# A planned attention-and-MLP kernel: an earlier copy of S, recalibrated load times, key products on two engines, and a new order

## The chip, the cores and the metric

The kernel runs on one core of a Trainium2 chip. A core has a matrix engine (TensorE, PE in the profile; its weight loads are PEld), a vector engine (VectorE, DVE), an activation engine (ScalarE, ACT), GpSimd (POOL) and SyncE (SP), which here only issues transfers. Each engine works through its own queue in order; the engines wait for each other by semaphores. SBUF is the working memory of 128 partitions, PSUM the eight banks that TensorE writes to. The metric is the device time of one execution in microseconds (us).

## What is computed

For each of 4 batches and 4 heads (1088 tokens, head size 32), `phi` turns a query or key into 64 products of two 8-wide projections, and attention is linear in them; a two-matrix MLP with a leaky relu follows.

```python
a = einsum('rd,bhsd->bhsr', S1, x);  b = einsum('rd,bhsd->bhsr', S2, x)      # r = 8
phi(x) = (a_i * b_j), 64 values per token
kv = phi(k)^T v;  z = sum over s of phi(k)
attn = phi(q) kv / (phi(q) z + 1e-6)
x = attn as 4352 tokens by 128
h = x @ w_in;  g = max(h, 0) + alpha * min(h, 0);  out = g @ w_out      # w_in 128x2048
```

## The kernel before

The kernel rewrites the MLP: the leaky relu is `alpha*h` plus `(1 - alpha)*relu(h)`. So `out = x @ W + relu(x @ w_in) @ w_out_bf`, with `W = (w_in * alpha) @ w_out` and `w_out_bf = (1 - alpha) * w_out`. Both are made in the opening: four blocks of w_in are transposed on TensorE (L403), multiplied with alpha on VectorE (L411) or ScalarE (L414) into `winT`, and 16 float32 matmuls (L421) add up W; `w_out_bf` is made in four blocks on GpSimd (L393) or ScalarE (L396), and `w_in_bf` in four casts on ScalarE (L385).

*Keys, per batch* (`keys`, L427): VectorE transposes k in two halves (`kT`, L434), TensorE multiplies with `Sk` (L442), VectorE transposes the result back (`ab`, L449). Then four products `phi` (L457; on VectorE for batch 0, on GpSimd for the others), a Gram block on TensorE (L471), from it `exs` (L478, L479), a small matmul with `G` (L481) and the copy of z into `Wq` (L483). `phi` and v give `kv` (L491), which is copied (`kvs`, L495), transposed (L502) and copied again (`kvw`, L504).

*Queries, in five units* (`queries`, L511; units 0 and 1 are batch 0): transposes of q (`qT`, L518), products with `Wq` (L527), four transposes (`qa`, L533), then the chain `ac` (L548), a sum (L550), plus epsilon (L553), reciprocal (L554), `an` (L555, qa times rd), two products `qf` (L562, called `p_` in the code), two transposes `qp` (L566), and the numerator on TensorE (L579). Unit 0 does this chain on VectorE, the others do the products on GpSimd. The numerator's four blocks are copied to `xT` (L588).

*MLP, in nine groups of 512 tokens* (`mlp`, L594; the last has 256): 16 matmuls with `w_in_bf` (L602), a relu each on ScalarE (L609) or VectorE (L611), 16 matmuls with `w_out_bf` (L615), one with W (L622), a transpose out of PSUM (L627) and four stores. A group needs the units that cover its tokens.

*Order.* Nothing loops at run time. Every piece of work is an `Op` with an engine (or several to choose from, with an estimated length each), a priority, what it depends on and which buffers it takes. `schedule` (L65) picks, again and again, the operation that can start first by its own estimates; among those within 60 ns the one of lowest priority number, from `PRIO` (L28). Loads are planned on one imaginary queue `DQ` with the lengths given to `load` (L316). `SLACK` is added to waits between engines, `STICK` favours staying with one shape on TensorE. The resulting list only sets the order in each engine's queue; at run time an instruction starts when its data and buffer are there and its engine is free. Before TensorE has useful work it multiplies zeros (`zeros`, L352): 16 matmuls first, then fillers that the planner puts into gaps. Loads of later batches stand behind one-element memsets on VectorE (`gate`, L331), so that they start when a given piece of the earlier batch is done.

Of the kernel before, what the change touches and what calls it, by code (L numbers as in the profile page):

```python
# [25 lines left out]

SLACK = {"ACT": 0, "PE": 120, "DVE": 80}
PRIO = {"W": -25831, "wm": -16185, "win": 2590, "wo": -34520, "k": [-30754, -2740, -58459, -37449], "v": [-24647, -6543, 39476, 61086], "q": [-69891, -35754, -36540, -9190, 57445], "d": [-53704, -20334, -22485, -17259, 4159]}  # L28

# [19 lines left out]
class Op:  # L49
    def __init__(self, eng, fn, prio, deps=(), takes=(), frees=(), lat=190, ni=2, cfg="full", glue=None):  # L50
# [3 lines left out]
        self.takes, self.lat, self.ni, self.cfg, self.glue = list(takes), lat, ni, cfg, glue  # L54
# [6 lines left out]
SWITCH, COLD, FILL = 95, 6600, 14000  # L61
STICK = {"PE": 22100}


def schedule(ops, slots, filler=None):  # L65
# [4 lines left out]

    free_at = {"DVE": 900, "PE": 1000, "POOL": 700, "ACT": 700}
    cfg, glued = "full", None
# [19 lines left out]
    while ready:  # L92
        best = None
        known = {}
        for o in ready:
# [43 lines left out]
        if e == "PE" and filler and 4000 < free_at.get(e, 0) < FILL:  # L139
# [4 lines left out]
            if n > 0 and idle:  # L144
# [30 lines left out]
def kernel(  # L175
# [52 lines left out]
    Wq = [sb(f"Wq{b}", [128, 32]) for b in range(B)]  # L228
    oma = sb("oma", [128, NC])
    warm = sb("warm", [128, 256], BF16)  # L230
    kvw = [sb(f"kvw{b}", [128, 2, 128]) for b in range(B)]
# [40 lines left out]
    def dve(n):  # L272
        return (62 + n) / 0.96
# [64 lines left out]


    c_ident = op(("POOL", 700), lambda: make_identity(nc, ident), -900)  # L340

# [18 lines left out]
    c_warm0 = op(("DVE", 300), lambda: nc.vector.memset(warm, 0.0), -950)  # L360
    c_warm = op(("PE", 8 * 427 + 80), lambda: zeros(8, "O"), -900, deps=[c_warm0], ni=32)
    h_rows = Hold(HBANKS)
    c_rt = op(("PE", 300), lambda: nc.tensor.transpose(
        bank[h_rows.got[0]][:, :2 * r], rows, ident[:2 * r, :2 * r]),
# [23 lines left out]
    for i in range(4):  # L388
        s = slice(4 * i, 4 * i + 4)

        def f_wo(e, s=s):
            if e == "POOL":
                nc.gpsimd.tensor_mul(w_out_bf[:, s], w_out_f[:, s], view(oma[:, s], [[1, 4], [0, 128]]))  # L393
# [3 lines left out]
        c_wo.append(op({"POOL": 1050, "ACT": 1180}, f_wo, PRIO["wo"] + i, deps=[L[f"wo{i // 2}"], c_om]))  # L397
    for i in range(4):
# [18 lines left out]
    wm = []  # L417
    for i in range(4):
        def f_wm(i=i):
            for c in range(4 * i, 4 * i + 4):  # L420
                nc.tensor.matmul(bank[hW.got[0]][:, :DM], winT[:, c], w_out_f[:, c], start=(c == 0), stop=(c == NC - 1))  # L421
        wm = [op(("PE", 1000), f_wm, PRIO["wm"] + i, deps=[c_wT[i], L[f"wo{i // 2}"]] + wm, takes=[hW] if i == 0 else [],
                 lat=250, ni=16)]
    c_W = op(("ACT", 250), lambda: nc.scalar.copy(W_bf, bank[hW.got[0]][:, :DM]), PRIO["wm"] + 10, deps=wm, frees=[hW])


    def keys(b, prio, late):  # L427
# [25 lines left out]
        for rr_, h2 in ((0, 0), (0, 1), (1, 0), (1, 1)):  # L453
            def f_ph(e, rr_=rr_, h2=h2):
# [4 lines left out]
                               view(src, [[64, KW], [0, r], [1, r]], 32 * rr_ + 16 * h2 + r))  # L459
            e = {"DVE": dve(KW * R)} if PHI_DVE[b] else {"POOL": 50 + KW * R * 2}  # L460
            ph.append(op(e, f_ph, prio + 3, deps=[t2[rr_]] + ph[:1], takes=[hph] if not ph else [], frees=[hab]))

        hz, hE, hC = Hold(banks), Hold(P_ex), Hold(banks)

        def f_gram():

            for w in (0, 5, 1, 6, 2, 7, 3, 8, 4):
# [4 lines left out]
                                 stop=w in (4, 8), skip_group_check=True)  # L472
        zb = op(("PE", 620), f_gram, prio + 3, deps=t2, takes=[hz], frees=[hab], lat=250, ni=36, cfg="128x64")

# [36 lines left out]
    def queries(u, b, starts, nb, end, prio, late, z_op, kv_op):  # L511
# [34 lines left out]
        def rd():  # L546
            return bufs[hrd.got[0]][:, :H * nb]
        ac = op(("POOL", 170 + 2 * n) if slow else ("DVE", dve(n) + 130), lambda e: side(e).tensor_mul(part(2), part(2), part(0)),  # L548
                prio + 3, deps=ta)
        sm = op(("DVE", dve(n) + (30 if slow else 120)), lambda: nc.vector.reduce_sum(rd(), part(2), axis=mybir.AxisListType.X), prio + 3,  # L550
# [4 lines left out]
        an = op(("POOL", 150 + 1.8 * n) if slow else ("DVE", dve(n) + 130), lambda e: side(e).tensor_mul(  # L555
            part(0), part(0), view(bufs[hrd.got[0]], [[1, H * nb], [0, r]])), prio + 3, deps=[rc], frees=[hrd])
        hqf, hqp = [Hold(P_qf) for _ in range(2)], [Hold(P_qp) for _ in range(2)]
        mu = []
        for rr_ in range(2):
            def f_p(e, rr_=rr_):  # L560
# [3 lines left out]
                                   view(src, [[32, 2 * nb], [0, r], [1, r]], 2 * n * rr_ + r))  # L564
            p_ = op(("POOL", 60 + 1.9 * 4 * n) if slow else ("DVE", dve(4 * n)), f_p, prio + 4, deps=[an], takes=[hqf[rr_]], frees=[hqa])
            mu.append(op(("DVE", dve(4 * n) + 40), lambda rr_=rr_: nc.vector.transpose(  # L566
                bufs[hqp[rr_].got[0]][:, :4 * n], bufs[hqf[rr_].got[0]][:, :4 * n]),
                prio + 5, deps=[p_], takes=[hqp[rr_]], frees=[hqf[rr_]]))
# [122 lines left out]
```

## Time and profile before

| | |
|---|---|
| median of 3 runs | 111.69 us (110.04 to 111.81) |
| the profiled execution | 109.54 us, of which the span from first to last instruction is 107.5 us |
| granted TensorE clock | 1.00 |
| relus on ScalarE / VectorE | 107 / 37 |
| phi of batch 0 on VectorE / GpSimd | 4 / 0 |
| w_out_bf blocks on GpSimd / ScalarE | 2 / 2 |

The page has one line for each engine (busy time, share of the span, instructions), a view of the span in 40 slices, the transfers, the chain of waits that ended last, and the costliest groups of instructions. A group's row gives line, engine, operation, what is written from what (buffer numbers left out), count, then busy time and mean ns of one, then the engine's idle time just before, with what ended it. A row of the timeline gives start, length, engine, line, operation, count, and in brackets the idle time before it and what released it. An instruction's recorded length includes its run-out, so that one may start while the one before it is still shown.

### The profile page before, as it was taken

To read this page: it belongs to the slowest core of one execution; us is meant where nothing else is said; L and a number is where in the kernel's file an instruction comes from. 1 tells how busy PE (TensorE), PEld (TensorE's weight loads), DVE (VectorE), ACT (ScalarE), POOL (GpSimd) and SP (SyncE) were. 2 spreads that over 40 slices of the span, in tenths; PEclk is the share of its full clock that TensorE was granted. 3 is DMA by queue.
4 is the path that set the end of the run, shared out by engine and by line. 5 is a ranking of instruction groups with operands and counts; after the bars stand their busy time and mean duration, and the time that the engine had idled before them with its cause. 6 is when DMAs were issued, how large, how long until landed. Compare 5 with 4: busy or idle time off the path is not lost.

```text
span 107.5 us, 3253 instructions
## 1 busy us (share of the span) xinstructions
PE 101.0 (94%) x1309; PEld 53.9 (50%) x1309; DVE 75.1 (70%) x160; ACT 70.7 (66%) x158; POOL 37.6 (35%) x41
## 2 busy tenths in 40 slices
PE   6969999999999999999999999999999899999960
PEld 4638889444546334456443444644454344444740
DVE  2559999897898879699568965885753444564740
ACT  0046889669760499336985974796769599496730
POOL 4000330089879996019993024930000000000000
PEclk9999999999999999999999999999999999999999
DMA  2999870796600288803550320420041060023143
GB/s 62 340 252 402 297 269 6 224 201 206 207 9 0 60 186 155 326 6 51 107 154 3 56 45 0 64 34 6 12 67 18 0 97 7 0 46 61 26 71 49
DMA packets 22863, 11.24 MB, mean 105 GB/s; under 512 B 19008, under 2 KB 21056, under 8 KB 22848
## 3 DMA queue, kind: packets, MB, share of 16 engines
q1 hardware_dynamic: 21952, 10.95, 39.5%
q8 instruction: 10, 0.16, 0.7%
q10 hardware_dynamic: 896, 0.08, 0.6%
q14 instruction: 5, 0.04, 0.2%
HBM read 8.80 MB, written 2.23 MB: 103 GB/s over the span
## 4 chain that ended last, share of the span: by engine, by line
PE 88%; DMA 4%; ACT 2%; DVE 1%; SPq 1%; issue 1%; ACTq 0%
PE O L615 27%; PE H L602 26%; PE A L579 6%; DMA q_sb<-in_q_dram 4%; PE H L421 4%; PE A L602 3%; PE A L527 3%; PE A L471 2%; PE A L491 2%; PE H L491 2%; PE O L355 2%; PE H L442 2%; PE O L622 2%; PE H L403 1%; PE A L442 1%; ACT rh L609 1%
## 5 line engine op out<-in xcount | busy, mean ns | idle before, releaser
L609 ACT ACTIVATE rh<-H 128x512 bf16<-128x512 f32 (+1 forms) x91 | 48.2, 593 | 10.5 <-PE H L602 10.2
L615 PE MATMUL O<-rh,w_out_bf 128*128 128x512 bf16 (+1 forms) x144 | 40.4, 367 | 0.0
L602 PE MATMUL H<-xT,w_in_bf 128*128 128x512 bf16 (+1 forms) x124 | 38.7, 374 | 0.6 <-ACT rh L609 0.6
L611 DVE TENSOR_SCALAR rh<-H 128x512 bf16<-128x512 f32 (+1 forms) x33 | 21.3, 652 | 9.7 <-PE H L602 8.1
L615 PEld LDWEIGHTS <-w_out_bf 128*128 128x128 bf16 x144 | 13.9, 97 | 17.6 <-issue 5.7
L602 PEld LDWEIGHTS <-w_in_bf 128*128 128x128 bf16 x144 | 13.3, 98 | 15.9 <-issue 3.3
L457 POOL TENSOR_TENSOR phi<-ab 128x576 f32<-128x576 f32 x12 | 13.8, 1177 | 13.1 <-DVE ab L449 13.1
L562 POOL TENSOR_TENSOR qf<-qa 128x1152 f32<-128x1152 f32 (+1 forms) x8 | 15.5, 1952 | 0.2
L627 DVE STREAM_TRANSPOSE oT<-O 128x512 f32<-128x512 f32 (+1 forms) x9 | 6.1, 680 | 9.3 <-PE O L622 9.2
L566 DVE STREAM_TRANSPOSE qp<-qf 128x1152 f32<-128x1152 f32 (+2 forms) x10 | 11.2, 1124 | 0.7 <-POOL qf L562 0.7
L609 ACT ACTIVATE rh<-A 128x512 bf16<-128x512 f32 (+1 forms) x16 | 7.1, 505 | 3.2 <-PE A L602 2.9
L355 PE MATMUL O<-warm 128*128 128x256 bf16 x42 | 7.5, 342 | 1.1 <-DVE warm L360 1.1
L434 DVE STREAM_TRANSPOSE kT<-k_sb 128x544 f32<-128x544 f32 x8 | 5.5, 716 | 2.7 <-DMA k_sb<-in_k_dram 2.7
L533 DVE STREAM_TRANSPOSE qa<-A 128x288 f32<-128x288 f32 (+2 forms) x20 | 6.7, 386 | 0.7 <-PE A L527 0.7
L579 PE MATMUL A<-qp,kvw 32*32 32x288 f32 (+2 forms) x320 | 7.0, 364 | 0.0
L588 ACT CAST xT<-A 128x256 bf16<-128x256 f32 (+3 forms) x12 | 3.4, 345 | 5.3 <-PE A L579 5.3
L518 DVE STREAM_TRANSPOSE qT<-q_sb 128x544 f32<-128x544 f32 (+2 forms) x10 | 5.9, 608 | 0.5 <-DMA q_sb<-in_q_dram 0.5
L355 PEld LDWEIGHTS <-warm 128*128 128x128 bf16 x42 | 4.9, 122 | 2.5 <-DVE warm L360 1.1
L393 POOL TENSOR_TENSOR w_out_bf<-w_out_f,oma 128x512 bf16<-128x512 f32 x2 | 2.1, 1042 | 10.8 <-DMA w_out_f<-in_moe_w_out_dram 10.7
L371 ACT ACT_TABLE_LOAD x1 | 1.3, 1283 | 6.7 <-DVE ST L366 6.7
L385 ACT CAST w_in_bf<-w_in_f 128x512 bf16<-128x512 f32 x4 | 4.6, 1157 | 1.0 <-DMA w_in_f<-in_moe_w_in_dram 1.0
L579 PEld LDWEIGHTS A<-qp,kvw 32*32 32x32 f32 x320 | 3.9, 103 | 2.5 <-issue 1.3
(86 smaller groups left out, 92.8 us busy)
## 6 DMA issues: line engine op xcount, KB each, us to landing
k_sb<-in_k_dram SPq DMA_DIRECT2D x3, 544.0 KB, 4.1
q_sb<-in_q_dram SPq DMA_DIRECT2D x3, 544.0 KB, 3.2
out_dram<-oT SPq DMA_DIRECT2D x20, 64.0 KB, 2.0
v_sb<-in_v_dram SPq DMA_DIRECT2D x8, 144.0 KB, 4.2
v_sb<-in_v_dram SPq DMA_DIRECT2D x8, 128.0 KB, 4.6
w_in_f<-in_moe_w_in_dram SPq DMA_DIRECT2D x2, 512.0 KB, 6.1
w_out_f<-in_moe_w_out_dram SPq DMA_DIRECT2D x2, 512.0 KB, 5.8
k_sb<-in_k_dram SPq DMA_DIRECT2D x2, 272.0 KB, 3.1
```

Of the source, the lines that this page charges most:

```text
L355: nc.tensor.matmul(bank[name][:, :256], warm[:, :128], warm[:, :256], start=True, stop=True)
L457: eng.tensor_mul(bufs[hph.got[0]][:, rr_, :, h2].rearrange("p w (i j) -> p w i j", i=r), view(src, [[64, KW], [1, r], [0, r]], 32 * rr_ + ...
L518: tq.append(op(("DVE", dve(32 * (x1 - x0))), lambda x0=x0, x1=x1: nc.vector.transpose(bufs[hqT.got[0]][:, 32 * (x0 - j0):32 * (x1 - j0)], ...
L533: ta.append(op(("DVE", dve(n)), lambda h=h: nc.vector.transpose(bufs[hqa.got[0]][:, h * n:(h + 1) * n], bank[hA[h].got[0]][:, :n]), prio + ...
L562: side(e).tensor_mul(bufs[hqf[rr_].got[0]][:, :4 * n].rearrange("p (m i j) -> p m i j", i=r, j=r), view(src, [[32, 2 * nb], [1, r], [0, r] ...
L566: mu.append(op(("DVE", dve(4 * n) + 40), lambda rr_=rr_: nc.vector.transpose(bufs[hqp[rr_].got[0]][:, :4 * n], bufs[hqf[rr_].got[0]][:, :4 ...
L579: nc.tensor.matmul(bank[hX[c].got[0]][32 * h:32 * (h + 1), :n], kvw[b][32 * c:32 * (c + 1), i, 32 * h:32 * (h + 1)], view(bufs[hqp[h // 2] ...
L602: hm = op(("PE", n / 2.4 + 3), lambda c=c, hh=hh: nc.tensor.matmul(bank[hh.got[0]][:, :n], w_in_bf[:, c * 128:(c + 1) * 128], xT[:, col0:c ...
L609: nc.scalar.activation(bufs[hr.got[0]][:, :n], bank[hh.got[0]][:, :n], ACTF.Relu)
L611: nc.vector.tensor_scalar_max(bufs[hr.got[0]][:, :n], bank[hh.got[0]][:, :n], 0.0)
L615: nc.tensor.matmul(bank["O"][:, :n], w_out_bf[:, c], bufs[hr.got[0]][:, :n], start=state["n"] == 0, stop=state["n"] == last)
L627: ev = op(("DVE", dve(n)), lambda: nc.vector.transpose(bufs[ho.got[0]][:, :nb].rearrange("p a b -> p (a b)"), bank["O"][:, :n]), prio - 5, ...
```

## The change

It makes these edits at once. The planner gets a new rule: operations marked `port` on VectorE and GpSimd are never planned at the same time as each other. The marks are on `w_out_bf`, `phi`, `ac`, `an` and `p_`. For batch 0 `phi` may be planned on either engine, and for unit 0 `p_` too. The memset of `warm` is planned first, and ScalarE copies 8 columns of it to a new tile `tab`, which nothing reads: its activation table is loaded there. W's 16 matmuls become eight operations of two (they were four of four). Planned lengths change for several loads (w_in's first from 2900 to 1500 ns), the Gram block, `phi` and the transpose of S; so do `SLACK`, `STICK`, the times at which engines are taken to begin, and all of `PRIO`. The list of dependencies of `w_out_bf` on unit 0's last `p_` (a rule for the planner only) goes.

```diff
-SLACK = {"ACT": 0, "PE": 120, "DVE": 80}
-PRIO = {"W": -25831, "wm": -16185, "win": 2590, "wo": -34520, "k": [...], ...}
+SLACK = {"ACT": 80, "PE": 60, "DVE": 30}
+PRIO = {"W": -2429, "wm": -2407, "win": -2437, "wo": -610, "k": [...], ...}
...
-STICK = {"PE": 22100}
+STICK = {"PE": 1000}
...
-    free_at = {"DVE": 900, "PE": 1000, "POOL": 700, "ACT": 700}
+    free_at = {"DVE": 830, "PE": 900, "POOL": 700, "ACT": 700}
...
+                if o.port and e in ("DVE", "POOL"):
+                    t = max(t, free_at.get("PORT", 0))
...
+        if o.port and e in ("DVE", "POOL"):
+            free_at["PORT"] = end
...
-    load("k0a", 1600, lambda: l_k(0, 0, 17))
+    load("k0a", 1750, lambda: l_k(0, 0, 17))
...
-    load("v0", 2200, lambda: l_v(0))
-    load("wi0", 2900, lambda: l_win(0))
-    load("wi1", 1400, lambda: l_win(1))
-    load("wo0", 1400, lambda: l_wout(0))
-    load("wo1", 1400, lambda: l_wout(1))
+    load("v0", 2500, lambda: l_v(0))
+    load("wi0", 1500, lambda: l_win(0))
+    load("wi1", 1300, lambda: l_win(1))
+    load("wo0", 1350, lambda: l_wout(0))
+    load("wo1", 1350, lambda: l_wout(1))
...
+    c_warm0 = op(("DVE", 60), lambda: nc.vector.memset(warm, 0.0), -950)
+    c_tab = op(("ACT", 1300), lambda: nc.scalar.copy(tab, warm[:, :8]), -940, deps=[c_warm0])
...
-    for i in range(4):
+    for i in range(8):
         def f_wm(i=i):
-            for c in range(4 * i, 4 * i + 4):
+            for c in range(2 * i, 2 * i + 2):
                 nc.tensor.matmul(bank[hW.got[0]][:, :DM], winT[:, c], w_out_f[:, c], start=(c == 0), stop=(c == NC - 1))
...
-            e = {"DVE": dve(KW * R)} if PHI_DVE[b] else {"POOL": 50 + KW * R * 2}
-            ph.append(op(e, f_ph, prio + 3, deps=[t2[rr_]] + ph[:1], takes=[hph] if not ph else [], frees=[hab]))
+            e = {"DVE": dve(KW * R), "POOL": 1200} if PHI_DVE[b] else {"POOL": 1200}
+            ph.append(op(e, f_ph, prio + 3, deps=[t2[rr_]] + ph[:1], takes=[hph] if not ph else [], frees=[hab], port=True))
...
-            p_ = op(("POOL", 60 + 1.9 * 4 * n) if slow else ("DVE", dve(4 * n)), f_p, prio + 4, deps=[an], takes=[hqf[rr_]], frees=[hqa])
+            p_ = op(("POOL", 60 + 1.9 * 4 * n) if slow else {"POOL": 60 + 1.9 * 4 * n, "DVE": dve(4 * n)}, f_p, prio + 4, deps=[an],
+                    takes=[hqf[rr_]], frees=[hqa], port=True)
...
-        if not slow:
-
-            for x in c_wo:
-                x.deps.append(p_)
```

What the planner makes of it, by the instructions in each engine's queue. In the opening VectorE now copies `ST`, `Sk` and `Y` directly after the two halves of `kT` and ahead of the transposes of q; it does one `phi` of batch 0 (behind `exs`) and GpSimd three; it copies `kvs` between the reciprocal and `an`. GpSimd's three `phi` are followed by three blocks of `w_out_bf`; ScalarE does one, behind its four casts of w_in, two blocks of `winT` and `kvw`. TensorE runs 4 fillers (not 6) ahead of the first key products, 6 and 6 (not 10 and 8) around the Gram block, and puts 12 of W's matmuls before unit 0's numerator and 4 behind it. Then come unit 1's query products and the first MLP matmul, and behind it batch 1's key products, which stood before both. Further on, unit 1's numerator follows all of group 0 and is followed by batch 2's key products and batch 1's `kv`; unit 2's numerator stands inside group 1 instead of behind it. ScalarE has 97 relus and VectorE 47.

More of the change, by code (lines that the diff above doesn't have):

```diff
@@ L49, with __init__ @@
 class Op:
-    def __init__(self, eng, fn, prio, deps=(), takes=(), frees=(), lat=190, ni=2, cfg="full", glue=None):
+    def __init__(self, eng, fn, prio, deps=(), takes=(), frees=(), lat=190, ni=2, cfg="full", glue=None, port=False):
         self.eng = eng if isinstance(eng, dict) else dict([eng])
@@ L53, in __init__ @@
         self.deps = [d for d in deps if d is not None]
-        self.takes, self.lat, self.ni, self.cfg, self.glue = list(takes), lat, ni, cfg, glue
+        self.takes, self.lat, self.ni, self.cfg, self.glue, self.port = list(takes), lat, ni, cfg, glue, port
         for h in frees:
@@ L229 @@
     oma = sb("oma", [128, NC])
+    tab = sb("tab", [128, 8])
     warm = sb("warm", [128, 256], BF16)
@@ L359, in filler @@
         return Op(("PE", each * n), lambda: zeros(n, name), 0, takes=[h], frees=[h], ni=4 * n)
-    c_warm0 = op(("DVE", 300), lambda: nc.vector.memset(warm, 0.0), -950)
     c_warm = op(("PE", 8 * 427 + 80), lambda: zeros(8, "O"), -900, deps=[c_warm0], ni=32)
     h_rows = Hold(HBANKS)
-    c_rt = op(("PE", 300), lambda: nc.tensor.transpose(
+    c_rt = op(("PE", 100), lambda: nc.tensor.transpose(
         bank[h_rows.got[0]][:, :2 * r], rows, ident[:2 * r, :2 * r]),
@@ L396, in f_wo @@
                     nc.scalar.mul(w_out_bf[:, c], w_out_f[:, c], oma[:, c:c + 1])
-        c_wo.append(op({"POOL": 1050, "ACT": 1180}, f_wo, PRIO["wo"] + i, deps=[L[f"wo{i // 2}"], c_om]))
+        c_wo.append(op({"POOL": 1050, "ACT": 1180}, f_wo, PRIO["wo"] + i, deps=[L[f"wo{i // 2}"], c_om], port=True))
     for i in range(4):
@@ L417 @@
     wm = []
-    for i in range(4):
+    for i in range(8):
         def f_wm(i=i):
-            for c in range(4 * i, 4 * i + 4):
+            for c in range(2 * i, 2 * i + 2):
                 nc.tensor.matmul(bank[hW.got[0]][:, :DM], winT[:, c], w_out_f[:, c], start=(c == 0), stop=(c == NC - 1))
-        wm = [op(("PE", 1000), f_wm, PRIO["wm"] + i, deps=[c_wT[i], L[f"wo{i // 2}"]] + wm, takes=[hW] if i == 0 else [],
-                 lat=250, ni=16)]
+        wm = [op(("PE", 480), f_wm, PRIO["wm"] + i, deps=[c_wT[i // 2], L[f"wo{i // 4}"]] + wm, takes=[hW] if i == 0 else [],
+                 lat=250, ni=8)]
     c_W = op(("ACT", 250), lambda: nc.scalar.copy(W_bf, bank[hW.got[0]][:, :DM]), PRIO["wm"] + 10, deps=wm, frees=[hW])
@@ L472, in f_gram @@
                                  stop=w in (4, 8), skip_group_check=True)
-        zb = op(("PE", 620), f_gram, prio + 3, deps=t2, takes=[hz], frees=[hab], lat=250, ni=36, cfg="128x64")
+        zb = op(("PE", 730), f_gram, prio + 3, deps=t2, takes=[hz], frees=[hab], lat=250, ni=36, cfg="128x64")
         def f_ex():
@@ L555, in queries @@
         an = op(("POOL", 150 + 1.8 * n) if slow else ("DVE", dve(n) + 130), lambda e: side(e).tensor_mul(
-            part(0), part(0), view(bufs[hrd.got[0]], [[1, H * nb], [0, r]])), prio + 3, deps=[rc], frees=[hrd])
+            part(0), part(0), view(bufs[hrd.got[0]], [[1, H * nb], [0, r]])), prio + 3, deps=[rc], frees=[hrd], port=True)
         hqf, hqp = [Hold(P_qf) for _ in range(2)], [Hold(P_qp) for _ in range(2)]
```

4 lines of the change are left out of this document (2 added, 2 removed).

## The prediction

> **What bounds the kernel now.** I read the page first, then the chain of waits, then the timeline of each engine through the opening.
>
> ```profile
> PE 101.0 (94%) x1309; PEld 53.9 (50%) x1309; DVE 75.1 (70%) x160; ACT 70.7 (66%) x158; POOL 37.6 (35%) x41
> ...
> PE 88%; DMA 4%; ACT 2%; DVE 1%; SPq 1%; issue 1%; ACTq 0%
> ```
>
> TensorE is busy all the time and is 88% of the chain, so time can be won in two ways only: useful matmuls begin sooner, or the stream of them has fewer pauses. 94% hides two different things, since part of TensorE's opening is filler on zeros. The opening on VectorE (start, length, instruction):
>
> ```profile
> 5.83 0.77 DVE L518 STREAM_TRANSPOSE qT<-q_sb 128x256 f32<-128x256 f32 x2 [0.51 <-DMA q_sb<-in_q_dram]
> 6.52 0.14 DVE L366 COPY ST<-H 128x16 f32<-128x16 f32 x1
> ...
> 7.70 0.48 DVE L449 STREAM_TRANSPOSE ab<-A 128x288 f32<-128x288 f32 x1 [0.68 <-PE A L442]
> ...
> 8.54 1.38 DVE L457 TENSOR_TENSOR phi<-ab 128x576 f32<-128x576 f32 x2
> 9.93 0.19 DVE L478 TENSOR_TENSOR exs<-A,pick 128x32 f32<-128x32 f32 x1
> ...
> 11.99 1.36 DVE L411 TENSOR_TENSOR winT<-H,al 128x512 f32<-128x512 f32 x2 [0.21 <-PE H L403]
> 13.26 0.90 DVE L533 STREAM_TRANSPOSE qa<-A 128x128 f32<-128x128 f32 x4
> 14.19 0.57 DVE L548 TENSOR_TENSOR qa<-qa 128x128 f32<-128x128 f32 x1
> ...
> 15.61 0.29 DVE L555 TENSOR_TENSOR qa<-qa,rd 128x128 f32<-128x128 f32 x1
> 15.94 1.29 DVE L562 TENSOR_TENSOR qf<-qa 128x512 f32<-128x512 f32 x2
> 17.16 1.29 DVE L566 STREAM_TRANSPOSE qp<-qf 128x512 f32<-128x512 f32 x2
> ```
>
> and on TensorE (filler L355, key products L442, W L421, numerator of unit 0 L579, query products L527, the first three MLP matmuls L602):
>
> ```profile
> 4.80 1.22 PE L355 MATMUL O<-warm 128*128 128x256 bf16 x6
> 6.94 0.72 PE L442 MATMUL A<-kT,Sk 64*32 64x288 f32 x16 [0.92 <-DVE Sk L368]
> ...
> 16.10 2.84 PE L421 MATMUL H<-w_out_f,winT 128*128 128x128 f32 x24
> 18.88 1.07 PE L579 MATMUL A<-qp,kvw 32*32 32x128 f32 x64
> 19.94 1.34 PE L442 MATMUL H<-kT,Sk 64*32 64x288 f32 x16
> 21.21 0.62 PE L527 MATMUL A<-qT,Wq 32*32 32x160 f32 x32
> 21.77 0.89 PE L602 MATMUL H<-xT,w_in_bf 128*128 128x512 bf16 x3
> ...
> 44.39 1.60 PE L579 MATMUL A<-qp,kvw 32*32 32x288 f32 x64
> ```
>
> VectorE hardly rests from 5.83 to unit 0's numerator at 18.88; that chain is the limit of the opening, and MLP work starts at 21.77. After it, the chain of waits gives the price of each TensorE block (start, share of the chain, what):
>
> ```profile
> 30.41 0.22 PE A L502 x2
> ...
> 31.06 0.65 PE A L442 x16
> ...
> 33.32 0.87 PE H L471 x18
> 34.19 1.13 PE A L579 x58
> 35.46 0.50 ACT xT L588 x2
> ...
> 37.13 0.61 ACT rh L609
> ...
> 47.16 1.28 PE H L491 x72
> ...
> 57.74 0.70 PE A L527 x32
> ...
> 96.41 3.24 PE O L615 x15
> ```
>
> An MLP matmul costs 3.24/15 = 0.216 us. From 21.77 to 44.39, 22.6 us, stand 65 of them (14.0), two Gram blocks (1.74), L491 1.28, two L527 (1.4), L442 0.65, L579 1.13, L502 0.22 and some 0.3 for L481: 20.7. So about 1.9 us of this stretch are pauses. The two ACT rows show 1.1 of them: between unit 1's numerator and group 1, TensorE waits for the copies of xT and then for the first relu. The other 0.8 are small waits for relus. The same count from 44.39 to the end gives about 3 us in pauses, none long.
>
> **The change part by part.** *S ahead of q.* S, its masked copy and Y leave the place behind two q transposes that wait for q's landing at 5.83, and follow the k transposes: 6.52 becomes about 5.25, and the first key products 6.94 becomes 5.67. TensorE then runs four fillers of the six (4.80 + 4 x 0.20 = 5.6), so it is free. The q transposes keep their landing. What is late next is w_in:
>
> ```profile
> 6.74 1.28 ACT L371 ACT_TABLE_LOAD   x1 [6.74 <-DVE ST L366]
> ...
> 9.71 1.14 ACT L385 CAST w_in_bf<-w_in_f 128x512 bf16<-128x512 f32 x1 [0.99 <-DMA w_in_f<-in_moe_w_in_dram]
> ```
>
> Its transposes cannot start before 9.71, and VectorE's winT products follow them, so of 1.27 us this part alone delivers none beyond that point. *Early table load* (the copy to tab): ACT waited 0.99 us for w_in anyway; worth 0, and 1.28 if that wait were gone.
>
> *Key products on two engines.* Three of four phi leave VectorE (3 x 0.69 = 2.07 us) and go to GpSimd:
>
> ```profile
> L457 POOL TENSOR_TENSOR phi<-ab 128x576 f32<-128x576 f32 x12 | 13.8, 1177 | 13.1 <-DVE ab L449 13.1
> ...
> L393 POOL TENSOR_TENSOR w_out_bf<-w_out_f,oma 128x512 bf16<-128x512 f32 x2 | 2.1, 1042 | 10.8 <-DMA w_out_f<-in_moe_w_out_dram 10.7
> ```
> ```profile
> 12.41 2.20 POOL L393 TENSOR_TENSOR w_out_bf<-w_out_f,oma 128x512 bf16<-128x512 f32 x2 [10.71 <-DMA w_out_f<-in_moe_w_out_dram]
> ```
>
> The first ab transpose moves from 7.70 to 6.55, behind the q transposes; the phi run from 7.0 to 7.0 + 3 x 1.18 = 10.5. L491, which needs them, stands behind three w_in transposes, the first of them at 9.71 or later, so they are hidden. But the two engines disturb each other. L548 and L555 have the same shape; L555 took 0.29, L548 0.57, and L548 ended at 14.76, just after GpSimd's second w_out product (12.41 + 2.20 = 14.61). I read this as VectorE standing still until GpSimd is through. The one phi left on VectorE stands behind the exs pair: second ab transpose done at 7.45, Gram block 0.9 and hand-over, exs and its sum 0.4, so 8.85. It starts at 9.35 or 10.5 (after GpSimd's second or third), the z copy of 0.15 follows at 10.05 to 11.2, the winT pair (not before 10.4, behind the first w_in transposes) takes 13.26 - 11.99 = 1.27, the qa transposes 0.93: L548 is due at 12.6 to 13.55, against 14.19.
>
> *w_out.* GpSimd now takes three of the four products, not two, and they start when w_out lands, at 12.41, in whatever place the planner put them: nothing else holds them back. Two took 2.20, 0.12 of it between them; three take 3.36. L548 and L555 both fall into that stretch. If VectorE gets its turn between two products: L548 ends at 13.75, the next two w_out products run to 15.95. From L548's end to L555 is 15.61 - 14.76 = 0.85 us, plus the copy of kvs, which moves from ScalarE to this place:
>
> ```profile
> L504 DVE COPY kvw<-A 128x256 f32<-128x256 f32 x2 | 0.8, 412 | 0.0
> ```
>
> 0.41: L555 asks at 15.0 and waits to 15.95, so the moved copy is hidden in that wait (and costs 0.41 without it). Then 0.33 + 1.22 + 1.23 as in the rows brings the numerator to 18.85, against 18.88. The bounds are 17.1, with no standing still (12.6 + 0.27 + 0.85 + 0.41 + 2.78, and a little for the start), and 20.0, where VectorE gets the turn only after all three. I take 18.85: it is nearest to the L548 row. [...] Who comes next when both queue, the trace doesn't show.
>
> *W two at a time.* Still 16 matmuls; four of them now stand behind the numerator: 4 x 2.84/12 = 0.95 that the early ones saved where TensorE waits anyway. So: numerator 18.85 + 1.06, W 0.95, L527 0.56: first MLP matmul at 21.4. Batch 1's key products, before it so far (19.94, stretched from 0.65 to 1.34 by a wait for the k transposes), come right after it: 21.4 + 0.65 = 22.05 against 21.77. **The opening loses 0.3.** ScalarE, with four w_in casts first, then two winT blocks, a copy and one w_out block, ends at 9.71 + 7 x 1.14 + 0.4 = 18.1 if none is longer than the cast shown, before xT is due at 19.9: 0. The table of p_'s engines keeps both on VectorE: 0.
>
> *New order.* Behind unit 1's numerator now stand L442 and L491 of the next batches, 0.65 + 1.28 = 1.93 us, ahead of group 1's first two matmuls, and the Gram block behind those. ScalarE's four xT copies (0.50 for two in the row) end inside, so the 1.1 us of waits go; next to be late is VectorE's Gram operand (below). I keep the 0.8 of small waits: **gain 1.1**, bounds 0 and 1.9. *Relus:* by the instruction order ScalarE has 97 instead of 107, VectorE 47 instead of 37. Of the late 3 us I give this 0.5, **bounds -0.7** (the longer VectorE relu delays its transposes) **and 1.2**.
>
> Sum: -0.3 + 1.1 + 0.5 = 1.3 us off 107.5 of span and off the profiled execution's 109.54: 108.2. That execution is the lowest of the four shown; the median of runs is 111.69, the mean of all four 110.8.
>
> **The rivals.** *No standing still* (L548 was long for another reason): numerator 17.1, 1.75 earlier, total 3.05. For it: only one instruction shows the disturbance. Against: it ends with GpSimd to within 0.15 us.
> *GpSimd keeps the turn* while its queue is full: numerator 20.0, total gain 0.15. For it: no row shows VectorE getting in between two queued GpSimd instructions. Against: two w_out leave 0.12 us between them.
> *VectorE becomes the bound*, and the kernel gets slower. Place: from unit 0's last qp transpose (18.73) to batch 2's ab transposes, which the Gram block behind group 1's first two matmuls needs.
>
> ```profile
> 19.00:36.00 17.00, 16.88 (x374) 8.52 (x372) 15.06 (x43) 10.47 (x27) 13.01 (x14) 1.00 0.48 135
> ```
>
> (Busy times of PE, PEld, DVE, ACT, POOL.) VectorE was at 15.06 of 17. The 38 instructions that the changed order puts there come, at the spacing of the same ones in this stretch, to 15.1 us, with 0.55 of waits for L527 to 34.35. TensorE arrives at 21.4 + 33 x 0.216 + 0.65 + 0.87 + 0.15 + 0.70 + 0.3 of small waits = 31.2, then 1.13 + 1.93 + 0.43 = 34.7. Some 0.3 us are spare. If each of the 38 costs 0.07 more, 2.7 in all, TensorE loses 2.4 and the kernel is slower by 1.1. It decides from 0.3 + 1.3 = 1.6 us of lateness on.
>
> **How the numbers follow.** Chances: the sum 0.52, no standing still 0.20, GpSimd keeps the turn 0.14, VectorE bound 0.09, anything else 0.05. From the mean of four, 110.8 - 1.3 = 109.5, which is the forecast; from the median it would be 110.4, from the profiled one 108.2. Range: low 110.8 - 3.05 - 0.5 = 107.2; high 110.8 + 1.1 = 111.9. The sum's own range (opening as taken, bounds of the other terms) is 108.1 to 111.0. 2%, about what a measurement of this kernel can tell, is 2.2 us, or 109.46 against the median. The sum lies at that edge, because the median was the high end of the four: I give it 0.38 of being beyond, no standing still 0.95, the turn kept 0.10: 0.20 + 0.19 + 0.01 = 0.40 faster. Slower by over 2%: half of VectorE bound and some of the rest, 0.06. Within: 0.54.
>
> **What would show it.** The first key products at 5.7 and GpSimd's phi from 7.0 show the first step. The qa,rd product ending just after a w_out product shows the standing still; a numerator at 17 refutes it, at 20 the turn was kept. TensorE without a pause of over 0.3 us behind unit 1's numerator shows the new order's gain; a wait of the Gram block for ab there shows the VectorE rival. I am wrong if the opening ends far from 21.4, or if pauses after 44 change by over 1 us.

## The result, and the profile after

| | kernel before | changed kernel |
|---|---|---|
| median of 20 runs each | 111.12 us (109.44 to 113.42) | 108.82 us (108.2 to 110.76) |
| the profiled execution | 109.54 us, span 107.5 | 109.73 us, span 107.7 |

The ratio is 0.9871, 95% interval [0.9831, 0.9911]: faster, by less than 2%, some 1.4 us. The medians stand further apart (108.82 / 111.12 = 0.979, 2.3 us), because the ratio leaves out the long executions, and the kernel before has more of them: of 47 that ran beside the experiments, 17 had a mean granted TensorE clock under 0.99 and a median of 111.73 us, the other 30 a median of 109.96; of the changed kernel's 20 none was under 0.993.

The two profiled executions mislead as a pair, for they took equally long. The one before would be the second lowest of that kernel's 20 runs, the one after is the fifth highest of its own. So the profile after answers how each step went, not by how much the kernel gained. Its page (busy time of each engine; then the engines' shares of the chain of waits):

```profile
PE 99.5 (92%) x1289; PEld 53.2 (49%) x1299; DVE 80.2 (74%) x166; ACT 66.9 (62%) x146; POOL 42.5 (40%) x45
...
PE 67%; DMA 16%; DVE 10%; ACT 1%; issue 1%; SPq 1%; ACTq 1%; DVEq 0%
```

TensorE's share of the chain went from 88% to 67%, in favour of transfers and VectorE. The pieces of the chain (start, length, what) say which:

```profile
4.21 6.35 DMA w_in_f<-in_moe_w_in_dram
10.60 0.73 PE H L410 x4
11.35 1.29 DVE winT L418 x2
...
16.53 1.29 DVE qf L569 x2
17.83 1.21 DVE qp L574 x2
19.09 5.74 DMA q_sb<-in_q_dram
24.86 1.37 DVE qT L525 x2
```

Up to unit 0's numerator the chain is w_in's landing and then VectorE; after it, the landing of batch 1's queries, a transfer issued at 19.09. The opening on VectorE (line numbers are those of the changed kernel: `ac` L555, +eps L560, `an` L562):

```profile
5.09 0.14 DVE L373 COPY ST<-H 128x16 f32<-128x16 f32 x1
...
6.70 0.77 DVE L525 STREAM_TRANSPOSE qT<-q_sb 128x256 f32<-128x256 f32 x2 [1.12 <-DMA q_sb<-in_q_dram]
...
8.13 1.01 DVE L386 TENSOR_SCALAR oma<-al 128x16 f32<-128x16 f32 x1
...
9.60 1.26 DVE L464 TENSOR_TENSOR phi<-ab 128x576 f32<-128x576 f32 x1
...
13.49 0.96 DVE L555 TENSOR_TENSOR qa<-qa 128x128 f32<-128x128 f32 x1
...
14.81 0.57 DVE L560 TENSOR_SCALAR rd<-rd 128x16 f32<-128x16 f32 x1
...
15.86 0.63 DVE L562 TENSOR_TENSOR qa<-qa,rd 128x128 f32<-128x128 f32 x1
```

and GpSimd, then TensorE:

```profile
7.92 3.97 POOL L464 TENSOR_TENSOR phi<-ab 128x576 f32<-128x576 f32 x3 [6.23 <-DVE ab L456]
13.27 3.08 POOL L400 TENSOR_TENSOR w_out_bf<-w_out_f,oma 128x512 bf16<-128x512 f32 x3 [1.37 <-DVE qa L540]
```
```profile
5.76 1.11 PE L449 MATMUL A<-kT,Sk 64*32 64x288 f32 x16
...
18.59 1.43 PE L583 MATMUL A<-qp,kvw 32*32 32x128 f32 x64 [0.37 <-DVE qp L574]
19.96 1.16 PE L428 MATMUL H<-w_out_f,winT 128*128 128x128 f32 x8
21.05 0.55 PE L534 MATMUL A<-qT,Wq 32*32 32x160 f32 x32
21.85 0.72 PE L449 MATMUL H<-kT,Sk 64*32 64x288 f32 x16 [0.25 <-issue]
22.61 0.38 PE L606 MATMUL H<-xT,w_in_bf 128*128 128x512 bf16 x1
...
32.51 1.18 PE L583 MATMUL A<-qp,kvw 32*32 32x160 f32 x64
33.61 0.72 PE L449 MATMUL H<-kT,Sk 64*32 64x288 f32 x16
34.12 1.32 PE L498 MATMUL H<-phi,v_sb 64*32 64x64 f32 x72
35.38 0.60 PE L606 MATMUL H<-xT,w_in_bf 128*128 128x512 bf16 x2
...
42.94 1.60 PE L583 MATMUL A<-qp,kvw 32*32 32x288 f32 x64
```
```profile
21.96 0.60 ACT L613 ACTIVATE rh<-H 128x512 bf16<-128x512 f32 x1 [0.54 <-PE A L534]
```

The row at 22.61 is not the first MLP matmul. In the changed order that one stands ahead of batch 1's key products, and its record is missing: the profile has 144 weight loads at L606 but 142 matmuls, the first load is at 21.53, and the relu at 21.96 already reads a result. So the first MLP matmul ran at about 21.63, in the 0.25 us that the row at 21.85 shows as "issue", and 22.61 is the second.

Three things are to be seen. First, q landed at 6.70, not 5.83, and w_in at 10.58, not 9.71 (4.21 + 6.35 by the chain gives 10.56); the change leaves the order of these loads as it was. Second, three VectorE instructions beside GpSimd's products are long: `oma` 1.01 (0.13 in the profile before), `ac` 0.96 and +eps 0.57, against 0.29 and 0.17 for the same shapes alone in the profile before. Third, behind unit 1's numerator TensorE runs on.

### The profile page after: what moved, and what is told of

It reads as the page before. It is cut to its first block, busy times and chain, and to the rows that moved or that the text cites. A ratio compares the mean times of both kernels' runs of the same rounds, so it can differ in the third digit from the quotient of the medians.

```text
span 107.7 us, 3221 instructions
## 1 busy us (share of the span) xinstructions
PE 99.5 (92%) x1289; PEld 53.2 (49%) x1299; DVE 80.2 (74%) x166; ACT 66.9 (62%) x146; POOL 42.5 (40%) x45
## 4 chain that ended last, share of the span: by engine, by line
PE 67%; DMA 16%; DVE 10%; ACT 1%; issue 1%; SPq 1%; ACTq 1%; DVEq 0%
PE O L619 25%; PE H L606 23%; DMA w_in_f<-in_moe_w_in_dram 6%; DMA q_sb<-in_q_dram 5%; PE A L583 5%; DMA rows<-in_S_dram 3%; PE A L606 2%; PE H L498 2%; PE A L534 2%; DMA out_dram<-oT 2%; PE A L478 2%; PE O L626 1%; DVE qT L525 1%; DVE qf L569 1%; PE H L449 1%; DVE winT L418 1%
## 5 line engine op out<-in xcount | busy, mean ns | idle before, releaser
L613 ACT ACTIVATE rh<-H 128x512 bf16<-128x512 f32 (+1 forms) x82 | 44.8, 593 | 14.2 <-PE H L606 12.8
L606 PE MATMUL H<-xT,w_in_bf 128*128 128x512 bf16 (+1 forms) x122 | 37.0, 374 | 0.6 <-ACT rh L613 0.3
L619 PE MATMUL O<-rh,w_out_bf 128*128 128x512 bf16 (+1 forms) x136 | 36.9, 366 | 0.4
L615 DVE TENSOR_SCALAR rh<-H 128x512 bf16<-128x512 f32 (+1 forms) x42 | 27.3, 661 | 5.5 <-PE H L606 4.3
L606 PEld LDWEIGHTS <-w_in_bf 128*128 128x128 bf16 x144 | 13.4, 98 | 17.0 <-issue 4.7
L464 POOL TENSOR_TENSOR phi<-ab 128x576 f32<-128x576 f32 x15 | 17.8, 1213 | 8.4 <-DVE ab L456 8.4
L363 PE MATMUL O<-warm 128*128 128x256 bf16 x32 | 6.3, 364 | 1.1 <-DVE warm L345 1.1
L555 POOL TENSOR_TENSOR qa<-qa 128x288 f32<-128x288 f32 (+1 forms) x4 | 2.9, 726 | 7.8 <-DVE qa L540 7.8
L592 ACT CAST xT<-A 128x128 bf16<-128x128 f32 (+3 forms) x13 | 3.6, 333 | 3.8 <-PE A L583 3.8
L363 PEld LDWEIGHTS <-warm 128*128 128x128 bf16 x32 | 3.8, 128 | 2.3 <-DVE warm L345 1.1
L562 POOL TENSOR_TENSOR qa<-qa,rd 128x288 f32<-128x288 f32 (+1 forms) x4 | 2.5, 630 | 5.9 <-DVE rd L561 5.0
```

The costliest lines, as they stand in the source:

```text
L363: nc.tensor.matmul(bank[name][:, :256], warm[:, :128], warm[:, :256], start=True, stop=True)
L464: eng.tensor_mul(bufs[hph.got[0]][:, rr_, :, h2].rearrange("p w (i j) -> p w i j", i=r), view(src, [[64, KW], [1, r], [0, r]], 32 * rr_ + ...
L606: hm = op(("PE", n / 2.4 + 3), lambda c=c, hh=hh: nc.tensor.matmul(bank[hh.got[0]][:, :n], w_in_bf[:, c * 128:(c + 1) * 128], xT[:, col0:c ...
L613: nc.scalar.activation(bufs[hr.got[0]][:, :n], bank[hh.got[0]][:, :n], ACTF.Relu)
L615: nc.vector.tensor_scalar_max(bufs[hr.got[0]][:, :n], bank[hh.got[0]][:, :n], 0.0)
L619: nc.tensor.matmul(bank["O"][:, :n], w_out_bf[:, c], bufs[hr.got[0]][:, :n], start=state["n"] == 0, stop=state["n"] == last)
```

## The experiments

Theory at first: S ahead of q is what the runs gain, with the rest about even. Rivals: the early table load; the new order; w_in. In the edits, `order` is the planner's finished list, and `moved` (a helper) puts operations at another place in it; nothing else changes unless it is told.

**The changed kernel again, and without the table load.**

> The changed kernel once more, for a second profile. In the profile of it shown so far q landed at 6.70 us (5.83 in the profile of the kernel before) and w_in at 10.56 (9.71), and the opening ended 0.84 later. If landings vary from one execution to the next, this profile shows q and w_in at other times and the first MLP matmul moves with w_in one for one. If the changed kernel itself delays its loads, they land at 6.7 and 10.6 again.

```diff
+    order = [x for x in order if x[2] is not c_tab]
```

> The changed kernel without the copy to tab, so that the activation table is loaded at the first copy to Wq, as before. Early load harmless (the sum as predicted): same time as the changed kernel, ratio to the kernel before 0.987. Rival, the early table load shares the transfer engines with k and q and delays q and w_in by 0.85 us: q lands near 5.8 and the time falls by some 0.8 us, ratio 0.980.

The changed kernel's second profile took 109.95 us: q at 6.80, w_in at 11.07, unit 0's numerator at 19.07, the second MLP matmul at 23.08 (22.61 in the first). So the landings vary and the opening moves with w_in. The change is not what makes w_in late: in the two profiles of the old order that follow, it came at 10.53 and 10.91, and the 9.71 of the profile before was an early landing. Without the load: 108.91 us median of 6 (108.14 to 109.41), ratio 0.9867 [0.9797, 0.9936], as with it; w_in at 10.38, numerator at 18.38. The early table load is worth nothing that can be measured. In these three profiles of the changed order the numerator starts 8.0 us behind w_in's landing.

**S, alone late and alone early.** The changed kernel with the first turn of q back in front of S; and the kernel before with S, Sk and Y in front of it.

```diff
+    order = moved(order, tag['tq0'], before=c_st)       # in the changed kernel
+    order = moved(order, tag['tq0'], after=c_y)         # in the kernel before
```

> The changed kernel with the two q transposes put back ahead of the copy of S. As predicted (what is late next is w_in): the key chain slips by 1 to 2 us but only 0.3 to 0.9 of it passes w_in's landing, ratio 0.990 to 0.995. Rival, the gain over the kernel before comes mostly from S no longer waiting for q's landing, which varies: all of it goes, ratio 0.998 or more, and the times spread as widely as those of the kernel before (109.4 to 113.4).

> The kernel before with one edit: the copy of S, Sk and Y ahead of the two q transposes. As predicted: some of 1.27 us arrives, but W's matmuls keep TensorE busy to 18.9 us, so 0.3 to 0.6 us, ratio 0.995 to 0.997. Rival (S waiting for q's landing is most of it): 1.3 us or more, ratio 0.988 or less, and a narrow spread.

S late: 110.92 us median of 6 (107.76 to 112.23), as long as the kernel before beside it (110.98), so that in most runs all of the change's gain is given back. No ratio comes of these six: five are long, three of them with mean clocks of 0.951 to 0.982 and two (110.91 and 112.15) with 0.997 and more, for which there is no profile and the cause stays open; the sixth, 107.76, is below every run of the changed kernel, so that S late does not cost time in every execution. S early in the old order: 109.43 us median of 12 (109.13 to 110.15); ratio 0.9945 [0.9899, 0.999]. The ratio puts the step at 0.6 us, near the top of what was expected as predicted; the medians put it at 1.55, and with the narrow spread that is the rival. The two differ by the long executions, which S early does not have. The profile with S late shows how one comes about. The page's row of granted clock, in tenths, 2.7 us to a digit, then TensorE, then busy times of PE, PEld, DVE, ACT and POOL in two stretches, with the granted clock ahead of the last two numbers:

```profile
PEclk9985589999999999999999999999999999999999
```
```profile
7.85 1.22 PE L450 MATMUL A<-kT,Sk 64*32 64x288 f32 x16 [2.71 <-DVE Sk L376]
...
9.27 1.48 PE L364 MATMUL O<-warm 128*128 128x256 bf16 x6
```
```profile
8.00:14.00 6.00, 6.00 (x51) 3.80 (x48) 3.29 (x7) 3.83 (x7) 4.18 (x4) 0.50 0.84 309
14.00:16.00 2.00, 2.00 (x44) 1.57 (x42) 1.50 (x5) 0.86 (x1) 2.00 (x3) 0.94 0.42 78
```

q landed at 6.74, S stood behind it, and TensorE, out of fillers, stood still for 2.71 us, to 7.85. From about 7.4 on its clock was halved (0.71 on the mean from 7 to 8, then 0.50): the six filler matmuls took 1.48 us, against 0.82 in the changed kernel. Half speed for 6.8 of 108.8 us makes a mean clock of 0.969, which is what that execution has. In the profile of before that the prediction read, q landed at 5.83, TensorE stood for 0.92 us, and the clock stayed at 1.00.

**The clock, apart from the chain.** The kernel before, S still late, with 16 more zero matmuls ahead of the first key products, so that TensorE does not stand.

```diff
+    x = filler(8, 'O', 110)
+    i = next(i for i, y in enumerate(order) if y[2] is tag['ab0'])
+    order = order[:i] + [(0, 'PE', x)] + order[i:]
```

> The kernel before with 16 more of the zero matmuls at L363 (256 columns each, about 2 us of TensorE) ahead of batch 0's first key products, so that TensorE does not stand idle while S waits behind q on VectorE; S stays late. Theory (S behind q costs time by way of the clock that TensorE is granted after standing still): no stretch of the opening under full clock, the time of most runs as with S early, 109.4 to 110.0, with a narrow spread, although the key products start no earlier. Rival (it costs by the chain itself, S to key products to unit 0): the median as before, near 111, whatever the clock.

Median of 10: 110.43 us (109.82 to 110.76), every mean clock at 0.994 or more; the kernel before ran beside it at 111.3 (109.29 to 112.39), seven of its 13 executions with a mean clock of 0.976 to 0.985. Ratio 1.0035 [0.9984, 1.0086]. Both theories hold a part. The ratio shows no gain, so the fillers help only by taking away the long executions: 0.9 us off the median and most of the spread. With S early the median is another 1.0 lower, at 109.43, and that is the chain itself (less some 0.15: in the profile the fillers ended at 7.30, Sk was ready at 7.15). The two parts come to more than 1.55 because the kernel before had 111.3 beside the one and 110.98 beside the other.

**w_in first.** If w_in's landing bounds the opening, its loads ahead of batch 0's values should help the changed kernel, and not the old order.

```diff
+    order = moved(order, [L['wi0'], L['wi1']], before=L['v0'])
```

> The changed kernel with w_in's two loads ahead of the first batch's values on SP. In the three profiles of the changed order that have S early, unit 0's numerator starts 8.0 us behind w_in's landing (10.38 and 18.38, 10.58 and 18.59, 11.07 and 19.07), because VectorE has winT's two products ahead of the turns of qa. Theory (w_in's landing bounds the opening of the changed kernel): w_in at 9.3 to 9.7, the numerator at about 17.5, the time 0.6 to 1.0 us below the changed kernel, a ratio to the kernel before of about 0.978 to 0.981. Rival (something else is late at once: the values of batch 0, which now land later, and with them L498 and kvw, or W's matmuls): the numerator stays within 0.3 us of 18.5, the ratio at 0.985 to 0.99.

> The kernel before with S's copies ahead of the turn of q, and w_in's two loads ahead of the first batch's values. Theory (in the old order it is not w_in's landing but TensorE's W matmuls ahead of the numerator that set the opening: 18.88 at a landing of 9.71, 18.84 at 10.53): the numerator stays within 0.3 us of 18.85 and the ratio within 0.003 of 0.9945, the run with S alone early. Rival (w_in bounds the old order as well, and the two profiles agreed by accident): the numerator 0.8 us earlier, the ratio about 0.987.

Both were slower: 111.96 us, ratio 1.0199 [1.0065, 1.0332]; and 113.06, ratio 1.0265 [1.0129, 1.0402]. TensorE in the first:

```profile
9.84 0.36 PE L489 MATMUL A<-exs,G 128*128 128x8 f32 x2 [0.82 <-DVE exs L487]
10.05 1.12 PE L411 MATMUL H<-ident,w_in_f 128*128 128x128 f32 x8
...
14.43 1.93 PE L499 MATMUL H<-phi,v_sb 128*32 128x64 f32 x64 [1.11 <-DMA v_sb<-in_v_dram]
...
20.47 1.44 PE L584 MATMUL A<-qp,kvw 32*32 32x128 f32 x64
```

w_in came at 9.79, 0.8 us earlier, but the values only at 14.4, and with them kv. VectorE waited for kv with the copy of kvs, which stands ahead of `an` in its queue:

```profile
16.45 0.42 DVE L503 COPY kvs<-H 128x256 f32<-128x256 f32 x1 [2.17 <-PE H L499]
```

The numerator came at 20.47; from 14 to 17 us the granted clock was 0.5. In the second, w_in came at 11.46, no earlier than without the edit (10.53), and alpha as late as 12.26 (1.67 + 10.59 by the chain). VectorE's queue stood behind `oma`, which needs alpha: TensorE waited 4.62 us at the Gram block. So neither run tests the theory: a load put first made another one last, and the second run's w_in was not even earlier. Of the two orders of loads the present one is the faster.

**GpSimd out of VectorE's way.** The changed kernel with `oma`, and so all of w_out's products, behind unit 0's last turn of qp.

```diff
+    order = moved(order, [c_om], after=tag['mu0'])
+    order = moved(order, pool, after=c_om)         # w_out's products on GpSimd
+    order = moved(order, act, after=pool[-1])      # and the one on ScalarE
```

> The changed kernel with oma, and with it all of w_out's products on GpSimd and ScalarE, behind unit 0's last turn of qp, so that no GpSimd product stands beside VectorE's ac, +eps and an. Theory (VectorE's time beside GpSimd is time on the path): these three return from 0.96, 0.57 and 0.63 us to about 0.30, 0.17 and 0.29, the numerator comes 0.7 to 1.0 us earlier for the same landing of w_in (7.1 to 7.4 us behind it, 8.0 in the changed kernel), and the time falls by 0.4 to 0.9 us, a ratio of 0.979 to 0.983. Rival (the products only move their cost: GpSimd now runs beside the turns of unit 1's queries and of batch 1's keys, or w_out comes too late for the MLP's second matmuls): the numerator earlier, but first MLP matmul or unit 1's numerator not, and the ratio within 0.003 of 0.987.

> The kernel of no_port once more, for a narrower interval. If its gain over the changed kernel is what its profile shows (unit 0's numerator 1.1 us earlier, unit 1's 2.15), the median is 107.0 to 107.8 and the ratio 0.968 to 0.980; if the one profile was a lucky execution, the ratio is 0.982 or more.

107.54 us median of 4, ratio 0.9778 [0.9656, 0.99]; again, 107.67 us of 6, ratio 0.9808 [0.9749, 0.9866]. VectorE and TensorE in the first:

```profile
13.38 0.29 DVE L557 TENSOR_TENSOR qa<-qa 128x128 f32<-128x128 f32 x1
...
14.03 0.17 DVE L562 TENSOR_SCALAR rd<-rd 128x16 f32<-128x16 f32 x1
...
14.69 0.28 DVE L564 TENSOR_TENSOR qa<-qa,rd 128x128 f32<-128x128 f32 x1
```
```profile
10.49 1.16 PE L411 MATMUL H<-ident,w_in_f 128*128 128x128 f32 x8 [0.59 <-DMA w_in_f<-in_moe_w_in_dram]
...
17.47 1.07 PE L587 MATMUL A<-qp,kvw 32*32 32x128 f32 x64
...
30.36 1.18 PE L587 MATMUL A<-qp,kvw 32*32 32x160 f32 x64
```

`ac`, +eps and `an` are back at 0.29, 0.17 and 0.28 us (2.16 together before, 0.74 now). w_in landed at 10.47, and the numerator came 7.0 us behind it, not 8.0. The products found free time behind the turns of qp, and the MLP did not wait for them. The disturbance was on the path, and taking it out is worth 1.2 us by the medians (108.82 to about 107.6).

**Unit 0's query products first.** The same kernel with batch 0's fourth key product on GpSimd too, the query products ahead of w_in's transposes, and the turns of qa ahead of winT.

```diff
+    order = [(x[0], 'POOL', x[2]) if x[1] == 'DVE' and x[2] in phi0 else x for x in order]
+    order = moved(order, [tag['fq0']], before=wt)   # w_in's first transposes
+    order = moved(order, tag['ta0'], before=wa)     # winT's first product
```

> The kernel of no_port with all four of batch 0's key products on GpSimd (so no conflict with VectorE's share of them, 1.26 us), unit 0's query products ahead of w_in's transposes and the turns of qa ahead of winT, so that TensorE has 0.5 us of useful work while it waits for w_in. Theory (in no_port TensorE works without a pause from w_in's landing to unit 0's numerator, and only work brought ahead of the landing counts): the numerator 6.4 to 6.6 us behind w_in's landing instead of 7.0, the time 0.3 to 0.6 us below no_port. Rival (a fourth product on GpSimd makes the key products end at 12.4 or later, and L499 with the copy of kvs is late instead): numerator 7 us behind the landing or more, the time as no_port's.

107.29 us median of 6 (106.76 to 107.92), ratio 0.9769 [0.9712, 0.9826], with the intervals of the two overlapping. Its numerator came 6.8 us behind w_in (11.07 and 17.84): a fifth of a microsecond where a half was expected. It is the fastest median measured, but not shown to be faster than the version without it.

**Batch 1's queries released earlier.** The two memsets that release these loads stand ahead of the second qf product instead of behind the turns of qp.

```diff
+    order = moved(order, L['q1'].deps[:1] + L['v1'].deps[:1], before=tag['p0'])
```

> The changed kernel with the two gates that release the loads of batch 1's queries and values (L337, 1x1 memsets on VectorE) ahead of unit 0's second qf product instead of behind its last turn of qp, some 1.8 us earlier on VectorE's queue; every other queue keeps its order. Theory (in the changed kernel batch 1's queries land too late, at 24.8, VectorE waits 1.03 us for them and TensorE loses 0.4 us behind that at L488 and some more in relus that VectorE holds): qT of batch 1 starts without a wait for the DMA, unit 0's numerator stays within 0.2 us for the same landing of w_in, unit 1's numerator comes 0.4 to 0.8 us earlier, 13.3 to 13.5 us behind unit 0's instead of 13.9; the time falls by as much, a ratio of 0.979 to 0.983. Rival (VectorE and TensorE make the wait good before unit 1's numerator, or the loads, released earlier, collide with others and land as late): unit 1's numerator as far behind unit 0's as in the changed kernel, ratio within 0.003 of 0.987.

109.54 us median of 10 (108.7 to 110.13), ratio 0.997 [0.9929, 1.001]: no gain, but 0.7 us more than the changed kernel's median. In the profile the wait for q is gone and unit 1's numerator stands 13.45 us behind unit 0's, as forecast, but the clock was halved from 11 to 14.5 us (0.52 on the mean from 11 to 14), after pauses of TensorE (0.78 and 1.05 us) that lie ahead of the edit, and unit 0's numerator came at 19.61; four of the ten executions had a mean clock under 0.993, and none of the changed kernel's 20; why this kernel has more of them was not found. Nor was the lateness steady: the next experiment, with the old release, had no wait for q, and 13.25 us; of the two profiles of no_port, one had no wait and 12.89, the other waited 1.00 and had 13.51. So a late q costs about 0.65 us where it happens; what an earlier release is worth in the median stays open.

**The new order's cover taken away.** Batch 1's kv (L498) behind group 1's first two matmuls and the Gram block.

```diff
+    order = moved(order, tag['kv1'], after=tag['zb2'])
```

> The changed kernel with batch 1's L498 (1.26 us of TensorE) behind group 1's first two MLP matmuls and the Gram block that follows them, so that only 0.65 us of key products cover the copies of xT and the first relu behind unit 1's numerator. Theory (the cover of 1.93 us is what the new order gains): TensorE pauses 0.4 to 1.0 us between unit 1's numerator and the Gram block, the distance from unit 1's numerator to unit 2's grows from 10.4 to 10.8 to 11.3, and the time by as much, a ratio of 0.991 to 0.996. Rival (the pauses are made good, since the same work is only turned round): distance within 0.2 of 10.4, ratio within 0.003 of 0.987.

110.96 us median of 4, ratio 1.0124 [1.0047, 1.0202]. TensorE behind unit 1's numerator:

```profile
31.80 1.18 PE L587 MATMUL A<-qp,kvw 32*32 32x160 f32 x64
32.91 0.72 PE L450 MATMUL H<-kT,Sk 64*32 64x288 f32 x16
34.47 0.74 PE L610 MATMUL H<-xT,w_in_bf 128*128 128x512 bf16 x2 [0.84 <-DVE ab L457]
...
37.90 0.44 PE L512 MATMUL A<-ident,kvs 128*128 128x128 f32 x2 [0.55 <-ACT kvs L505]
...
44.05 1.36 PE L587 MATMUL A<-qp,kvw 32*32 32x288 f32 x49
```

From numerator to numerator it is 12.25 us, 10.43 in the changed kernel: 1.8 more, and the median is 2.1 higher. The direction is the theory's, the size above the 0.4 to 0.9 it gave, because the edit opens a second pause: the transposes of kv, with nothing left between them and kv, wait 0.55 for the copy. The first, 0.84, is the cover that is gone. What it covers is not the copies of xT, as the prediction had it, but VectorE's turn of the key products, which frees the PSUM banks that group 1's matmuls write.

## Why the prediction was right in its range and wrong in its reason

Forecast 109.5, measured 108.82: inside the range, and within 2% by the ratio. Even the size agrees: the sum said 1.3 us off, the ratio says some 1.4. But that agreement is luck. On the scale on which the sum was made, profiled execution against profiled execution, the two came out 0.2 apart the other way; and of the runs' gain, 2.3 by the medians, most hangs on a step that the sum priced at nothing.

**S ahead of q: the step that failed.** The prediction says that "of 1.27 us this part alone delivers none beyond that point". The move went as written (first key products at 5.76; 5.67 forecast). Its price was taken from one execution, in which q came at 5.83, so that w_in seemed late next. For that one the price may hold: with S early in the old order the numerator came at 18.84, against 18.88, though w_in landed 0.8 later. But in the later profiles with the loads' order unchanged q came at 5.97 to 6.80. With S behind it that lengthens TensorE's idle stretch (0.92 us at 5.83; 2.71 at 6.74, with two fillers fewer), and in the long one the granted clock fell to 0.50. By the medians the step is worth 1.55 us in the old order (110.98 to 109.43) and 2.1 in the new one (110.92 to 108.82); in the old order 0.9 of it is what the fillers recover, with no mean clock under 0.994, and by the ratio, without the long executions, 0.6 is left. The prediction had the row that warned of it, 0.92 us of idle time ahead of the first key products, and did not ask what that becomes when q is late.

**The opening loses 0.3.** The first MLP matmul came at 21.63, forecast 21.4, and the end of batch 1's key products at 22.61. One MLP matmul (0.22) is done by then, so the number to hold against the forecast 22.05 and the 21.77 of before is 22.39: a loss of 0.62. By the 8.0 us from landing to numerator, w_in's landing, 0.87 later, is enough to make all of it. With the landing nearly equal, S early in the old order (10.53) had its first MLP matmul at 21.93 (by its weight load, for its record is missing too), and the changed kernel (10.58) stands 0.46 behind that. The forecast missed by 0.34 in small pieces: W's four matmuls behind the numerator took 1.09 us and not 0.95, the key products 0.76 and not 0.65, and the numerator ended 0.05 late (19.96 against 19.91). It came earlier than forecast, at 18.59, but took 1.37 and not 1.06, because it starts after the first turn of qp and its second half waits for the second.

**Standing still on VectorE.** Right in kind: `ac` ended at 14.45, one product of 1.03 us into GpSimd's stretch (13.27 + 1.03 = 14.30), and `an` at 16.49, just after its end (16.35). Here VectorE got its turn between two queued products, so both rivals fall, no standing still (17.1) and GpSimd keeps the turn (20.0); the numerator at 18.59 is near 18.85, though w_in landed 0.87 later than in the profile that the forecast was made from, so the nearness of the two numbers is in part luck. But the forecast had two instructions held up. The rows have five: `oma` (1.01 us, 0.13 alone) and `phi` (1.26, 0.69 alone) too, beside GpSimd's key products, and +eps (0.57, 0.17 alone). And the prediction was content with a numerator as late as before; no_port shows 1.2 us of the kernel's time in these waits.

**New order, gain 1.1.** From unit 1's numerator to unit 2's the kernel before takes 10.27 us with 33 MLP matmuls (7.14 at 0.216) and 2.03 of other blocks, the changed one 10.43 with 24 (5.20) and 5.04: pauses of 1.1 and 0.2, so **0.9** gained. The size was near, what is covered was not (kv_later).

**Relus, 0.5.** From unit 2's numerator to the end: 63.11 us before, 64.76 after with eight MLP matmuls more to do (1.73), so 63.03. **0.1**, inside the bounds.

**VectorE becomes the bound.** No: the Gram block behind group 1's first two matmuls did not wait. But between the numerators of units 0 and 1 a transfer was late that no step named: batch 1's queries, released by a memset that stands on VectorE behind unit 0's chain, 1.03 us of wait at 24.86.

The span grew by 0.2. With 0.62 lost in the opening and 0.9 and 0.1 gained behind unit 1's numerator, a loss of about 0.6 is left for the stretch in between, the one in which batch 1's queries were late; counted directly from 22.61, its 9.90 us hold 32 MLP matmuls (6.93) and 1.69 of other blocks, so pauses of 1.3, against 0.7 before (12.35 us with 32 and 4.71). The sum had no term for it.

## What to carry to other kernels

A price that hangs on when a transfer lands is not taken from one execution: ask what each wait becomes if the landing is a microsecond later, above all where TensorE stands behind it: in s_late the 2.71 us without a matmul came with a granted clock of 0.50 for about 6.8 us. Where a profile and the median of the runs disagree, first ask which end of the runs the profile is from. And where one VectorE instruction beside GpSimd is seen to be long, look for every other one: moving the small instruction that releases GpSimd's work behind VectorE's chain was worth 1.2 us by the medians, beside 2.3 for the whole change.

## What the runs showed of the hardware

*The clock.* In s_late TensorE had no matmul for 2.71 us, up to 7.85, and the granted clock was 0.50 for about 6.8 us (from 7.4 to 14.2). In q1_early, after pauses of 0.78 and 1.05 us within 4 us, it was 0.50 for about 3.4 us (11.1 to 14.5); in the changed kernel's second profile pauses of about the same length (1.0 and 0.8) left it at 1.00. (The ends are worked out from the mean clocks of 1 us stretches: 0.71 from 7 to 8 and 0.88 from 14 to 15 in s_late, 0.55 from 11 to 12 and 0.74 from 14 to 15 in q1_early.) Why one of two such openings lost clock and the other did not, these runs do not show.

*VectorE beside GpSimd.* In the changed kernel's first profile two one-input VectorE instructions on 16 elements per partition, from SBUF to SBUF, were long beside GpSimd's products, as two-input ones were: `oma` took 1.01 us and +eps 0.57, 0.13 and 0.17 alone in the profile before; `ac` took 0.96 and `an` 0.63, 0.29 and 0.28 in no_port. The sum and the reciprocal kept their length there (0.29 and 0.25, as in the profile before).
